# Moving GpSimd's copies of the global probabilities one slot on, and an output copy to an earlier place, in a fused attention and MoE kernel

## The chip, the cores and the metric

The kernel runs on one core of a Trainium2 chip. The metric is device time in microseconds (us) of one execution; the time before is 1080.44 us, the median of three runs (1079.32 to 1082.52). A core has five engines that run side by side, each through its own list of instructions in order: TensorE (PE, matmuls; its weight loads are PEld), VectorE (DVE), ScalarE (ACT), GpSimd (POOL), and SyncE (SP), which here only issues transfers (DMAs). They wait for each other by semaphores.

## The reference

```
def _attn_ref(q_l, k_l, v_l, q_g, k_g, v_g):       # B=8, H=8, 512 local and 32 global rows, D=64
    k_all = concat([k_g, k_l]); v_all = concat([v_g, v_l])
    out_g = softmax(scale * q_g @ k_all.T) @ v_all           # 32 global rows see all 544 keys
    s_ll = where(|i - j| <= 32, scale * q_l @ k_l.T, -1e9)   # local rows see a band
    s_lg = scale * q_l @ k_g.T                               # and the 32 global keys
    out_l = softmax(concat([s_lg, s_ll])) @ concat([v_g, v_l])
    return concat([out_g, out_l])
...
x = attention, as 4352 tokens x 512
out = (relu(x @ w_in) ** 2) @ w_out                # 512 -> 2048 -> 512
```

## The kernel before

The main loop (line 610) runs over 146 slots t. The first 128 slots each carry one half (256 local rows) of one head: scores on PE, a band softmax, a transpose of the probabilities, and their product with v. Slots t >= 9 also carry one eighth of an MoE block of 256 tokens: slot t works on step m = t - 9. A block is 8 steps; `gemm1(m)` makes 256 hidden columns, `act1` applies relu and square, and `gemm2(m-1)` adds the step before to two output tiles in PSUM (`o0` and `o1`), in two halves. So after each eighth step both output tiles must be emptied by `evac` (line 524) before the next `gemm2` may write them; this falls into slots with t % 8 = 2, in which `m % 8 == 1`. `evac` copies each tile with ACT to SBUF (`ot`) and sends it out. The copy of tile 0 goes into a buffer with the tag `ptl`, that of tile 1 into one with the tag `gvl`, and the global attention uses the same two buffers.

Most operands are split into a high and a low part of a rounded format, so that products take two or three matmuls; the low part is always a DVE subtraction of two SBUF tensors (`v`, `ph`, `ml`, `pl`, `qk`, `gvl`, `ptl`).

The probabilities of slot t are transposed by DMA. `turn(t)` (line 223) has POOL copy `prob` in three pieces to `planes`, low and high 16-bit halves apart, and SP issues a DMA transpose to `turned`. In slot t + 1, `join(t)` (line 231) has POOL put the halves together again in `joined`; `parts` (ACT, `ph`) and `parts_rest` (DVE: `ph`, `ml`, `pl`) split it, and PE multiplies (`av`, tile `xa`).

The rows of the global queries go the same way, for four heads at a time: 16 groups in all, two per 16 slots. Their scores are gathered in `sg` (128 rows x 640 columns: 544 keys, two repetitions of the last 32, and 32 of zeros). A group's work is spread over some eight slots by a table of jobs (line 685), each with a slot and a place in it. Before the change these are, counted from a slot d:

- d + 1: `g_soft` (DVE: row maximum) and `g_exp` (ACT)
- d + 2, place 3: `g_norm`: DVE repeats the 32 columns twice in `sg`, takes the reciprocal of the sum, and calls `g_turn`: one POOL copy of all of `sg` to `gp` (buffer tag `pth`), then a DMA transpose to `gq` (buffer tag `ptl`)
- d + 3, place 3: `g_split_v` (ACT `gvh`, DVE `gvl`), and `g_join`: one POOL copy of `gq` back to `sg`
- d + 4, place 3: `g_parts` (ACT `pth`, DVE `ptl` and the last part of `pth`); place 0: `g_av`, 13 matmuls to `gxo`, between the two halves of `gemm2`

d is 11 or 1 modulo 16. For d = 11 the slots of `g_norm`, `g_join` and `g_parts` are 13, 14 and 15 modulo 16; for d = 1 they are 3, 4 and 5.

From slot 17 on (`FREE`) every engine keeps the program order for what is issued through `pe`, `ve`, `ac`, `po` and `sp`; the planner puts the rest, among it the DMAs issued by `nc.sync` (the output, the global v and q), where it likes. In a slot POOL's order is: `join(t-1)`, `turn(t)`, then the jobs of place 3. ACT's is: `x_evac`, `split_v`, the two exponentials, `parts`, the jobs of place 3, `evac`, the split of the next q and k, `act1`, `act2`. SP's is: the transpose of `turn(t)`, the load of a later head, then a job's transpose.

Of the kernel before, what the change touches and what calls it, by code (L numbers as in the profile page):

```python
# [17 lines left out]
P = 128  # L18
# [9 lines left out]
NSTEP = NBLK * 8  # L28
# [10 lines left out]
def f(ap):  # L39
    return ap.bitcast(F32)  # L40
# [19 lines left out]
def attention_moe(  # L60
# [10 lines left out]
    pe, ve, ac, po, sp = (InOrder(tc, e) for e in (nc.tensor, nc.vector, nc.scalar, nc.gpsimd, nc.sync))  # L71
# [46 lines left out]
    sg = cp.tile([P, 2, 640], F32, name="sg")  # L118
# [36 lines left out]
    def scores(t):  # L155
        hd = heads[t]
        pool, tag = (ps_h, "h") if t < 8 and t % 2 else (ps_a, "s")
        s = pool.tile([P, 2, WIN], F32, tag=tag, name=f"s{t}")
        for u in range(2):
            qs, ks = slice(KC + u * P, KC + u * P + P), slice(128 * u, 128 * u + WIN)  # L160
            if plain(t):
                pe.matmul(s[:, u, :], hd["raw"][:, qs], hd["raw"][:, ks], start=True, stop=True)
            else:
                pe.matmul(s[:, u, :], hd["hi"][:, qs], hd["hi"][:, ks], start=True, stop=False)
                pe.matmul(s[:, u, :], hd["lo"][:, u * P : u * P + P], hd["hi"][:, ks], start=False, stop=True)
        hd["s"] = s
# [5 lines left out]
    def softmax1(t):  # L172
        hd = heads[t]
        hf = (t // 8) % 2
        pr = p2.tile([P, QK + QC], F32, tag="qk", name=f"pr{t}")[:, : 2 * WIN] if plain(t) else prob
        hd["pr"] = pr
        st = p2.tile([P, 8], F32, tag="st", name=f"st{t}")
        for u in range(2):
            m = 2 * hf + u
            ve.tensor_tensor_reduce(  # L180
                out=pr[:, WIN * u : WIN * (u + 1)],
                in0=hd["s"][:, u, :],
                in1=masks[:, WIN * m : WIN * (m + 1)],
                scale=-scale(t),
                scalar=3.0e38,
                op0=ALU.add,
                op1=ALU.min,
                accum_out=st[:, u : u + 1],
            )
        hd["st"] = st  # L190
# [40 lines left out]
    def join(t):  # L231
        words = joined.bitcast(U16).rearrange("p (n h) -> p h n", h=2)
        po.tensor_copy(words, turned.rearrange("p (h c) n -> p h (c n)", h=2))
# [44 lines left out]
    def x_evac(t):  # L278
        g, h = divmod(t, 8)
        xa = heads[t]["xa"]  # L280
        r = slice((h % 2) * 64, (h % 2) * 64 + 64)
        if g == 0:
            ac.copy(xg[r, h // 2, :], xa)
        else:
            ac.copy(x_h[r, g % 2, h // 2, :], xa)
            ve.tensor_sub(x_l[r, g % 2, h // 2, :], xa, f(x_h[r, g % 2, h // 2, :]))
        heads[t] = None
# [76 lines left out]

    def g_norm(t):
        s, st = sg[:, (t // 4) % 2, :], state["gst", t]
        for o in (544, 576):
            ve.tensor_copy(out=s[:, o : o + 32], in_=s[:, 512:544])
        ve.tensor_scalar(out=st[:, 3:4], in0=st[:, 2:3], scalar1=1e-9, scalar2=None, op0=ALU.add)
        ve.reciprocal(out=st[:, 0:1], in_=st[:, 3:4])  # L370
        ve.tensor_copy(out=st[:64, 1:2], in_=st[64:, 0:1])
        g_turn(t, s)

    def g_turn(t, s):

        a = p1.tile([P, 1280], U16, tag="pth", name=f"gp{t}")
        z = p1.tile([P, 10, P], U16, tag="ptl", name=f"gq{t}")
        words = s.bitcast(U16).rearrange("p (n h) -> p h n", h=2)
        po.tensor_copy(a.rearrange("p (h n) -> p h n", h=2), words)
        sp.dma_start_transpose(out=z, in_=a)  # L380
        state["gq"] = z

# [141 lines left out]
    def evac(blk, tiles=(0, 1)):  # L524
        for i in tiles:
            pool, tag = ((p1, "ptl"), (p1, "gvl"))[i]
            ot = pool.tile([P, DM], F32, tag=tag, name=f"ot{blk}_{i}")
            ac.copy(ot, moe["o"][i])
            if blk < NGR:
                b, hf = divmod(blk, 2)  # L530
                r0 = b * 544 + 32 + hf * 256 + i * P
                nc.sync.dma_start(out[r0 : r0 + P, :], ot)
            else:
                for bb in range(4):
                    r0 = (4 * i + bb) * 544
                    nc.sync.dma_start(out[r0 : r0 + 32, :], ot[32 * bb : 32 * bb + 32, :])
# [41 lines left out]
    def w_tick(t, place):  # L578
        if t < len(PLAN):
            for c in PLAN[t].split(",")[place]:  # L580
                {"b": w_pass, "s": w_chunk}[c]()
# [27 lines left out]
    jobs = {}  # L609
    for t in range(NSTEP + LAG + 1):  # L610
        m = t - LAG
# [10 lines left out]
            transposes(t - 1)  # L622
        if new:
            join(t - 1)
        if live and not early:
            scores(t)
        if old:
            pt_copy(t - 1)
        if NPLAIN <= t - 2 < NT:
            x_evac(t - 2)  # L630
        if live:
            softmax1(t)
        if run:
# [12 lines left out]
        for place in (4, 3):  # L646
            for job, *args in jobs.pop((t, place), ()):
                job(*args)
        if 0 < m <= NSTEP and m % 8 == 1 and m > 8:
            evac(m // 8 - 1)  # L650
        w_tick(t, 0)
        if live and early:
            g_scores(t)
# [29 lines left out]
        if live and t % 4 == 3 and (t // 8) % 2 == 1:  # L683
            d = t if t % 8 == 3 else t + 2
            for at, *job in (
                (d, 2, g_load_v, 0),
                (d + 1, 3, g_soft),
                (d + 1, 1, g_exp),
                (d + 2, 3, g_norm),
                (d + 3, 3, g_split_v, 0),  # L690
                (d + 3, 2, g_load_v, 1),
                (d + 3, 3, g_join),
                (d + 4, 3, g_parts),
                (d + 4, 0, g_av, 0),
                (max(d + 5, 17), 3, g_x, 0),
                (d + 5, 2, g_split_v, 1),
                (max(d + 6, 17), 0, g_av, 1),
                (max(d + 7, 18), 3, g_x, 1),
            ):
                place, job, *args = job  # L700
                jobs.setdefault((at, place), []).append((job, t, *args))
# [102 lines left out]
```

## Time and profile before

| | |
|---|---|
| median of the runs | 1080.44 us |
| the profiled execution | 1076.66 us |
| its span, first to last instruction | 1074.9 us |
| mean granted TensorE clock | 0.990 |
| PE busy | 1031.6 us (96%), 7040 matmul records |
| DVE busy | 853.1 us (79%) |
| ACT busy | 718.1 us (67%) |
| POOL busy | 382.1 us (36%), 496 instructions |

All times in the text are counted from the start of the span. "Busy" counts an engine's instructions from start to end, also where an instruction stands still because another engine holds something that it needs. Matmuls overlap and their ends are modelled, so the busy time of PE says less than the gaps and the lengths of the slots. A slot is measured here from the first matmul of `gemm1(m)` to that of the next step.

### The profile page before, as it was taken

The page shows a single profiled execution, that of the slowest core. Times are in us where ns is not written, and L with a number is a line of the kernel's source. Part 1 is how long each engine was busy: PE and PEld are TensorE (multiplying, and loading weights), DVE is VectorE, ACT ScalarE, POOL GpSimd, SP SyncE. Part 2 cuts the span into 40 slices and gives each one's busy share as a digit, 9 for nine tenths or more (in the row PEclk, how much of TensorE's full clock was granted, in tenths as well). Part 3 has the DMA queues.
Part 4 walks back from the last instruction along what each step waited for, and adds up shares of the span by engine and source line. Part 5 has one row for each costly group of instructions (what it writes and reads, how often), then busy time and mean ns, then how long its engine had stood idle before and what let it go on. Part 6 is the DMA issues. An engine that isn't in the chain of part 4 may idle for free.

```text
span 1074.9 us, 20570 instructions
## 1 busy us (share of the span) xinstructions
PE 1031.6 (96%) x7040; PEld 908.9 (85%) x7040; DVE 853.1 (79%) x2477; ACT 718.1 (67%) x1743; POOL 382.1 (36%) x496
## 2 busy tenths in 40 slices
PE   8999899999999999999999999999999999999998
PEld 6876788988988989888888989888888889889896
DVE  5689888888889878888879888888889888883211
ACT  6888667766767756767666766776667666664432
POOL 1010434444344443444335443453434343441000
PEclk9999999999999989999999999999999999999999
DMA  9772354545355444454445454445545453441000
GB/s 368 306 258 84 95 128 98 119 115 136 93 121 112 124 102 108 112 131 114 108 116 110 111 123 114 121 105 123 126 101 114 118 133 95 117 95 48 11 20 20
DMA packets 193576, 127.69 MB, mean 119 GB/s; under 512 B 143552, under 2 KB 168640, under 8 KB 193472
## 3 DMA queue, kind: packets, MB, share of 16 engines
q1 hardware_dynamic: 193328, 126.32, 45.8%
q8 instruction: 55, 0.90, 0.3%
q14 instruction: 49, 0.40, 0.1%
q10 hardware_dynamic: 144, 0.07, 0.0%
HBM read 82.84 MB, written 8.91 MB: 85 GB/s over the span
## 4 chain that ended last, share of the span: by engine, by line
PE 41%; DVE 30%; ACT 13%; issue 7%; DMA 5%; POOL 4%; POOLq 0%; SPq 0%; DVEq 0%; ACTq 0%
PE o L53 17%; PE h L53 16%; DVE qk L53 5%; ACT prob L53 5%; DVE prob L53 4%; DVE ml L53 4%; DMA turned<-planes 4%; PE xa L53 3%; PE s L53 3%; DVE gl L53 3%; POOL joined L53 2%; DVE st L53 2%; ACT ph L53 2%; DVE x_l L53 2%; POOL planes L53 2%
## 5 line engine op out<-in xcount | busy, mean ns | idle before, releaser
L53 PE MATMUL h<-x_h,ws 128*128 128x256 f32 x2048 | 395.6, 286 | 0.0
L53 PEld LDWEIGHTS h<-x_h,ws 128*128 128x128 f32 x2048 | 332.9, 194 | 0.7
L53 PE MATMUL o<-ws,gh 128*128 128x512 f32 x1024 | 323.9, 397 | 9.8 <-ACT ot L53 9.3
L53 PE MATMUL h<-x_l,ws 128*128 128x256 f32 x1024 | 293.0, 286 | 0.0
L53 POOL COPY joined<-turned 128x1024 uint16<-128x1024 uint16 x112 | 155.9, 1392 | 323.9 <-DMA turned<-planes 192.9
L53 POOL COPY planes<-prob 128x448 uint16<-128x448 uint16 x336 | 170.0, 543 | 211.6 <-DVE prob L53 211.6
L53 PEld LDWEIGHTS o<-ws,gh 128*128 128x128 f32 x1024 | 182.5, 188 | 44.7 <-ACT ot L53 12.8
L53 PE MATMUL o<-ws,gl 128*128 128x512 f32 x512 | 201.8, 394 | 0.0
L53 PEld LDWEIGHTS h<-x_l,ws 128*128 128x128 f32 x1024 | 199.3, 195 | 1.3 <-DVE x_l L53 0.2
L53 ACT ACTIVATE prob<-prob,st 128x224 f32<-128x224 f32 x224 | 106.3, 475 | 109.3 <-DVE st L53 109.2
L53 DVE TENSOR_TENSOR gl<-pt,gh 128x512 fp32r<-128x512 f32 x128 | 87.6, 684 | 75.9 <-ACT gh L53 75.2
L53 DVE TENSOR_TENSOR qk<-raw,qk 64x352 fp32r<-64x352 f32 x224 | 114.5, 511 | 7.5 <-ACT qk L53 0.6
L53 ACT CAST x_h<-xa 64x256 fp32r<-64x256 f32 x120 | 43.7, 364 | 113.5 <-PE xa L53 113.2
L53 PEld LDWEIGHTS o<-ws,gl 128*128 128x128 f32 x512 | 96.1, 188 | 22.8
L53 ACT ACTIVATE pt<-h 128x512 f32<-128x512 f32 x128 | 74.4, 581 | 57.0 <-PE h L53 56.3
L53 PE MATMUL s<-qk 128*128 128x224 f32 x448 | 85.9, 304 | 9.8 <-DVE qk L53 6.8
L53 ACT CAST ph<-joined 128x512 fp32r<-128x512 f32 x112 | 68.3, 610 | 27.7 <-POOL joined L53 26.9
L53 ACT CAST qk<-raw 128x608 fp32r<-128x608 f32 x112 | 78.3, 699 | 5.7 <-DMA raw<-in_pk_dram 5.3
L53 PEld LDWEIGHTS s<-qk 128*128 128x128 f32 x448 | 63.3, 194 | 20.4 <-DVE qk L53 19.7
L53 DVE CUSTOM_DVE_ANT_0 prob<-s,con 128x224 f32<-128x224 f32 x224 | 77.6, 382 | 3.3 <-PE s L53 1.3
L53 ACT ACTIVATE pt<-pt 128x512 f32<-128x512 f32 x128 | 74.5, 582 | 4.1
L53 ACT CAST gh<-pt 128x512 fp32r<-128x512 f32 x128 | 74.6, 583 | 2.4
(86 smaller groups left out, 1592.5 us busy)
## 6 DMA issues: line engine op xcount, KB each, us to landing
raw<-in_pk_dram SPq DMA_DIRECT2D x112, 400.0 KB, 3.5
wr<-in_w_dram SPq DMA_DIRECT2D x32, 512.0 KB, 7.9
gv<-in_vg_dram SPq DMA_DIRECT2D x32, 320.0 KB, 3.7
out_dram<-ot SPq DMA_DIRECT2D x32, 256.0 KB, 2.5
raw<-in_pk_dram SPq DMA_DIRECT2D x15, 432.0 KB, 8.4
qr<-in_qg_dram SPq DMA_DIRECT2D x31, 64.0 KB, 3.1
turned<-planes SPq DMA_TRANSPOSE x112, 3.1
out_dram<-ot SPq DMA_DIRECT2D x8, 64.0 KB, 1.7
```

Of the source, the lines that this page charges most:

```text
L53: r = method(*args, **kwargs)
```

## The change

Three things change. First, `g_turn` is no longer called by `g_norm`; it is a job of its own in slot d + 3, at a new place 6 at the head of the slot, right behind `join(t-1)` and ahead of `turn(t)`. `g_join` moves from slot d + 3, place 3, to slot d + 4, place 6. Second, DVE no longer repeats the 32 columns in `sg`; `g_turn` has POOL make four copies in place of one: the first 544 columns (both halves), the repeated columns once for each half by a read with a step of zero, and the last 32 columns. Third, `evac` is called once for each output tile: tile 0 behind `x_evac` and ahead of the softmax of the slot, tile 1 at the old place.

```
     def g_norm(t):
         s, st = sg[:, (t // 4) % 2, :], state["gst", t]
-        for o in (544, 576):
-            ve.tensor_copy(out=s[:, o : o + 32], in_=s[:, 512:544])
...
-        g_turn(t, s)
-
-    def g_turn(t, s):
+    def g_turn(t):
+
+        s = sg[:, (t // 4) % 2, :]
...
-        po.tensor_copy(a.rearrange("p (h n) -> p h n", h=2), words)
+        to = a.rearrange("p (h n) -> p h n", h=2)
+        po.tensor_copy(to[:, :, :544], words[:, :, :544])
+        for h in range(2):
+            twice = words[:, h, 512:544].unsqueeze(1).broadcast_to([P, 2, 32])
+            po.tensor_copy(to[:, h, 544:608].rearrange("p (k n) -> p k n", k=2), twice)
+        po.tensor_copy(to[:, :, 608:], words[:, :, 608:])
         sp.dma_start_transpose(out=z, in_=a)
...
             join(t - 1)
+        for job, *args in jobs.pop((t, 6), ()):
+            job(*args)
...
         if NPLAIN <= t - 2 < NT:
             x_evac(t - 2)
+        done = 0 < m <= NSTEP and m % 8 == 1 and m > 8
+        if done:
+            evac(m // 8 - 1, (0,))
         if live:
             softmax1(t)
...
-        if 0 < m <= NSTEP and m % 8 == 1 and m > 8:
-            evac(m // 8 - 1)
+        if done:
+            evac(m // 8 - 1, (1,))
...
                 (d + 2, 3, g_norm),
                 (d + 3, 3, g_split_v, 0),
                 (d + 3, 2, g_load_v, 1),
-                (d + 3, 3, g_join),
+                (d + 3, 6, g_turn),
+                (d + 4, 6, g_join),
                 (d + 4, 3, g_parts),
                 (d + 4, 0, g_av, 0),
```

## The prediction

> **What bounds the kernel now.** I read the page first: its busy times, then the groups for idle time of PE.
>
> ```profile
> span 1074.9 us, 20570 instructions
> PE 1031.6 (96%) x7040; PEld 908.9 (85%) x7040; DVE 853.1 (79%) x2477; ACT 718.1 (67%) x1743; POOL 382.1 (36%) x496
> L53 PE MATMUL o<-ws,gh 128*128 128x512 f32 x1024 | 323.9, 397 | 9.8 <-ACT ot L53 9.3
> ```
>
> PE is the bound on average, and its waits for the output copies `ot` come to 9.3 us. Next I cut the span into slots, since the average hides them. The columns of this view of stages are: stretch, its length, busy time of PE, PEld, DVE, ACT, POOL, granted clock, DMA share, GB/s.
>
> ```profile
> 296.93:303.88 6.95, 6.95 (x53) 6.37 (x51) 6.16 (x18) 4.99 (x15) 3.15 (x4) 1.00 0.31 83
> 303.88:311.75 7.87, 7.21 (x53) 6.40 (x51) 5.85 (x16) 5.51 (x14) 3.42 (x4) 1.00 0.53 130
> 325.68:333.25 7.57, 7.42 (x53) 6.51 (x51) 7.24 (x24) 5.36 (x15) 4.51 (x5) 1.00 0.48 101
> 333.25:341.76 8.51, 7.84 (x52) 6.52 (x51) 7.76 (x19) 5.15 (x12) 5.30 (x6) 1.00 0.68 141
> 341.76:349.51 7.75, 7.75 (x65) 7.13 (x64) 6.66 (x22) 5.70 (x16) 2.60 (x4) 1.00 0.44 106
> 364.34:371.74 7.40, 7.30 (x52) 6.47 (x51) 7.01 (x22) 6.32 (x16) 2.56 (x4) 1.00 0.62 141
> 371.74:379.35 7.61, 7.41 (x52) 6.51 (x51) 6.72 (x22) 5.47 (x14) 4.18 (x6) 1.00 0.51 132
> 379.35:389.59 10.24, 8.54 (x53) 7.04 (x51) 9.29 (x21) 5.15 (x12) 5.47 (x6) 0.92 0.59 129
> 389.59:399.65 10.06, 10.06 (x64) 9.44 (x64) 6.43 (x19) 5.46 (x14) 3.60 (x5) 0.74 0.40 102
> ```
>
> A slot without other work takes 6.95 us with PE full; with the 13 `gxo` matmuls 7.75 (row 5). Slots over that are: those with `evac` (7.87 and 7.40), and the two groups of slots with global work: 13 to 15 modulo 16 (rows 3 to 5; I call them stretch B) and 3 to 5 (the last three, stretch A). In rows 4 and 8 DVE is busy for 7.76 and 9.29 us, more than PE's own 6.95: there DVE sets the time. In row 9 PE ran at a clock of 0.74. The timeline of stretch B shows why DVE is slow:
>
> ```profile
> 319.69 1.64 POOL L53 COPY joined<-turned 128x1024 uint16<-128x1024 uint16 x1 [3.23 <-DMA turned<-planes]
> 320.63 0.73 DVE L53 TENSOR_SCALAR st<-st 128x2 f32<-128x2 f32 x1 [0.53 <-ACT prob L53]
> 330.28 1.64 POOL L53 COPY gp<-sg 128x1280 uint16<-128x1280 uint16 x1
> 330.84 1.92 DVE L53 TENSOR_TENSOR qk<-raw,qk 64x352 fp32r<-64x352 f32 x2
> 333.59 1.36 POOL L53 COPY joined<-turned 128x1024 uint16<-128x1024 uint16 x1 [1.67 <-DMA turned<-planes]
> 335.90 0.58 DVE L53 TENSOR_SCALAR prob<-prob,st 128x224 f32<-128x224 f32 x2
> 336.36 1.71 POOL L53 COPY planes<-prob 128x448 uint16<-128x448 uint16 x3 [1.41 <-DVE prob L53]
> 338.02 1.81 POOL L53 COPY sg<-gq 128x1280 uint16<-128x1280 uint16 x1
> 338.38 1.55 DVE L53 TENSOR_TENSOR ml<-joined,ph 64x128 fp32r<-64x128 f32 x1
> 340.30 0.98 DVE L53 TENSOR_TENSOR qk<-raw,qk 64x352 fp32r<-64x352 f32 x2
> 341.29 1.35 POOL L53 COPY joined<-turned 128x1024 uint16<-128x1024 uint16 x1 [1.45 <-DVE qk L53]
> 344.25 0.72 ACT L53 CAST pth<-sg 128x640 fp32r<-128x640 f32 x1
> 345.06 0.78 DVE L53 TENSOR_TENSOR ptl<-sg,pth 128x512 fp32r<-128x512 f32 x1 [0.21 <-issue]
> 346.27 0.22 PE L53 MATMUL gxo<-gvh,ptl 128*64 128x128 f32 x1
> ```
>
> A DVE instruction of this kind stands still until the POOL copy that is running ends. The `qk` pair takes 0.98 us alone and 1.92 while `gp` runs; the 64 x 128 `ml` takes 1.55 us and ends at 339.93, with `sg<-gq` ending at 339.83; even the two-column `st` stands until `joined` ends (321.36 after 321.33). So each long POOL copy of the global work costs DVE about 1 us wherever DVE has such work waiting.
>
> **The change, part by part.** *Output copies.* In slot 10 modulo 16, ACT and PE stand so:
>
> ```profile
> 304.74 0.49 ACT L53 ACTIVATE prob<-prob,st 128x224 f32<-128x224 f32 x1 [0.53 <-DVE st L53]
> 306.56 0.62 ACT L53 CAST ph<-joined 128x512 fp32r<-128x512 f32 x1 [0.78 <-POOL joined L53]
> 307.08 1.06 ACT L53 COPY ot<-o 128x512 f32<-128x512 f32 x2
> 307.71 0.73 PE L53 MATMUL o<-ws,gh 128*128 128x512 f32 x2 [0.66 <-ACT ot L53]
> 308.51 0.63 PE L53 MATMUL o<-ws,gh 128*128 128x512 f32 x2
> ```
>
> PE takes up `o0` at 307.71, when the first copy is done, and `o1` at 308.51. With tile 0 emptied three microseconds earlier, PE starts `o0` at once and `o1` when tile 1's copy, now first at 307.08, is done: 307.71 in place of 308.51, 0.80 us saved. In the other slot (7.40) all of the 0.45 over 6.95 goes. The moved copy (half of 1.06 us) falls into ACT's idle 0.53 before the exponentials, and the 0.78 before `ph` holds the rest; without that cover the softmax would start 0.5 us later and DVE with it. Over 7 slots of the first kind, 6 of the second and slot 18 (taken like the first) this makes 7 x 0.80 + 6 x 0.45 + 0.80 = 9.1; the page's row has 9.3, which I take. Bounds: 9.3, and 0 if DVE, which sets the time in the global slots that follow, takes it all back.
>
> *DVE's repeats and POOL's four copies.*
>
> ```profile
> 322.06 1.19 POOL L53 COPY planes<-prob 128x448 uint16<-128x448 uint16 x3 [0.73 <-DVE prob L53]
> L53 POOL COPY gp<-sg x16: 1253/1458/1729, 53.8 to 985.9; 128x1280 uint16<-128x1280 uint16 x16
> L53 POOL COPY sg<-gq x16: 1622/1801/2011, 58.3 to 990.3; 128x1280 uint16<-128x1280 uint16 x16
> L53 DVE COPY sg<-sg 128x32 f32<-128x32 f32 x32 | 8.3, 303 | 0.2 <-ACT sg L53 0.2
> ```
>
> DVE loses 2 x 0.303 = 0.6 us a group. Three copies of 896 elements together take 1.19 us undisturbed; at the 0.98 ns an element of one copy (1253 / 1280) they would take 0.88, so a further copy costs about 0.155. Four copies are then 1.25 + 3 x 0.155 = 1.72 us: the first 1.07 (1088 elements), the small ones 0.22 each. No row shows a read with a step of zero; between nothing extra and the cost of a copy of `sg<-gq` an element (1622 / 1280 = 1.27 ns) it is under 0.05 us, and I take nothing.
>
> *The moved copies, stretch B.* In slot 13 `gp` no longer meets `qk`: 0.94 us of DVE and the repeats go, `qk` ends in time, and the slot falls from 7.57 to 6.95. In slot 14 `joined` still runs 333.59 to 334.95, for its data land no earlier. DVE now reaches `v` before that and waits for it; `v` ends at 335.3. Then POOL's first copy holds the port until 336.4; `st`, which stood at about 335.3, goes behind it, and the three small copies alternate with `st` and the two scalings. These end at 337.6 in place of 336.48, and `planes` starts at 337.8, not 336.36: 1.4 later. The copy `sg<-gq` is gone from `ml` (-1.24), so `qk` ends where it did (341.1 against 341.28): slot 15 starts at 341.65, 0.1 earlier in all. But `planes` being 1.4 later, `turned` lands 1.4 later, and `joined` starts at 342.7, not 341.29. Now `g_join` comes behind it: 342.7 + 1.35, 0.35 for a waiting `v`, 1.65 for the copy, gives 346.05. Behind this wait, on ACT, `pth` and all that follows it in the slot (the split of q and k, relu, square), and on DVE `st`, the scalings and `ptl`: 346.05 + 0.2 + 0.2 + 0.65 for the softmax, then 0.78, gives 347.9. PE wants `ptl` at 346.27, less the 0.1: it waits 1.75. Stretch B: 23.83 (rows 3 to 5) - 0.1 + 1.75 = 25.5. Both ends: with no wait for `ptl` 23.7, and with the first copy held up by DVE as `joined` was in row 319.69 (1.64 for 1.35) twice over, 26.1.
>
> On SP the transpose of the group now stands ahead of that of `turn(t)` and of the head's load, where it stood behind both. It is issued at 337.8 and takes SP 1.33 us; the `planes` are done at 339.5, so the issue delays nothing; in the DMA engines it may (rival 3).
>
> *Stretch A* has the same edits, with more to lose in slots 3 and 4. I take it to last the same 25.5, for after the change the same chain (landing, `joined`, `g_join`, `pth`, `ptl`) ends last.
>
> ```profile
> sum 156.92, PE 145.95 PEld 128.17 DVE 132.78 ACT 96.38 POOL 75.39; mean PE 24.33 PEld 21.36 DVE 22.13 ACT 16.06 POOL 12.56
> sum 144.15, PE 138.11 PEld 121.04 DVE 130.58 ACT 97.01 POOL 72.79; mean PE 23.02 PEld 20.17 DVE 21.76 ACT 16.17 POOL 12.13
> ```
>
> These are the sums of six stretches A (from 248.91 on, 26.15 each) and six B (from 202.69 on, 24.03 each). A gains 0.65 six times, 3.9; its first, with the expert weights still to split, I set at 2.4, as the longest of the six (27.91, the last three rows of the stages, less 25.5). B loses 1.47 seven times, 10.3. **Sum:** -9.3 - 3.9 - 2.4 + 10.3 = -5.3 us against the profiled 1076.66 (span 1074.9 and 1.8 around it), 1071. The median of the runs is 3.8 higher than that execution, so I name 1075.
>
> **Rivals.** *1, much faster:* the copies fit into POOL's idle time. Row 336.36 has 1.41 us of it ahead of `planes`. If `st` goes ahead of the first copy, `planes` are not late and `qk` ends 1.2 earlier; `joined` comes at 341.3 and `g_join` ends at 344.65, `ptl` at 346.2 as before. Slot 15 starts at 340.4, PE wants `ptl` at 344.9 and waits 1.3: B is 340.4 - 325.68 + 7.75 + 1.3 = 23.8, bound by the landing, and A the same. That is -0.2 x 7 - 2.35 x 6 - 4.1 - 9.3 = -29, or 1051. For it: POOL is only 36% busy. Against it: in the rows above the waiting side always stood for a whole copy.
>
> *2, slower:* the clock. Row 8 has PE idle for 1.7 us (10.24 - 8.54), and in row 9 the clock fell to 0.74, which cost 2.3 us (10.06 against 7.75). Slot 333.25 with 0.67 us idle kept 1.00. The place is slots 5 and 15, the price 0.9 (mean of stretch A) to 2.3 us, and it decides from about 1.7 us of waiting for `ptl`, just what I get. At 1.3 in each of 14: +18, 1093. Against it: row 8's 1.7 us lay close together, and the waits here are split over two slots.
>
> The Trainium skill ("TensorE: Matmul & The Clock Gate", "Why this matters for your kernels") has the clock fall only after idle gaps of about 3 us, a whole window. By that rule this rival would give nothing, and the sum stays -5.3. This trace disagrees: 0.74 came behind 1.7 us.
>
> *3, slower:* the group's transpose, now ahead, delays `turned`.
>
> ```profile
> 554.41 1.39 POOL L53 COPY joined<-turned 128x1024 uint16<-128x1024 uint16 x1 [4.94 <-DVE prob L53]
> DMA to landing us min/median/max: 3.0/3.1/4.8
> DMA to landing us min/median/max: 2.9/4.8/6.1
> ```
>
> `turned` lands after 3.1 us (second row), at worst 4.8; `gq` (third row) alone 2.9, behind `turned` and a load 4.8. If the 1.9 of difference turns round, half of it, 0.9, goes into each wait for `ptl`: 14 x 0.9 = +12.6, 1088.
>
> **Numbers.** Forecast (1065 to 1083) 0.45, rival 1 0.2, rival 2 0.2, rival 3 0.15. Range 1049 to 1095: from rival 1 to rival 2, each with a little beyond. A change of 0.3%, 3.2 us, is about what a measurement can tell. Faster: 0.31 of the forecast, 0.2 and 0.02 = 0.53; same: 0.12 and 0.07 = 0.19; slower 0.28.
>
> **What would show it.** `o<-ws,gh` loses its wait for `ot`; `qk` and `ml` lose their 1.9 and 1.5; `st` or `prob` gain stretched instances; PE waits for `ptl` appear in slots 5 and 15, and slots 13 and 3 fall to 6.95. No wait for `ptl` would show rival 1, a clock under 0.9 in slots 5, 15 and after, rival 2; `turned` landing over 3.5 us, rival 3.

## The result, and the profile after

The changed kernel takes 1069.32 us (median of four runs, 1068.00 to 1071.19), the kernel before 1079.88 us in the runs that stand beside it. The ratio is 0.9899, with an interval of 0.9875 to 0.9923: about 10.6 us faster, where the prediction had 5.4 (1080.44 to 1075). The ratios leave out a few disturbed, slow executions, among them the profiled one of e5 below, which therefore has no column in the table of slots. The busy times of the kernel after, and the group in which PE's waits for the output copies stood:

```profile
PE 1029.5 (96%) x7040; PEld 902.3 (84%) x7040; DVE 867.7 (81%) x2445; ACT 721.5 (67%) x1743; POOL 385.0 (36%) x544
L53 PE MATMUL o<-ws,gh 128*128 128x512 f32 x1024 | 324.4, 398 | 3.2 <-ACT ot L53 3.0
```

PE's waits for `ot` fell from 9.3 to 3.0 us. DVE has 32 instructions fewer and is busy 14.6 us longer: its instructions stand still longer. The stages again, in the columns of the prediction (stretch, length, PE, PEld, DVE, ACT, POOL, granted clock, DMA share, GB/s): slots 10, 12, 13, 14, 15, then 2, 3, 4, 5 modulo 16 of the same round.

```profile
303.84:311.01 7.17, 7.17 (x52) 6.27 (x51) 5.85 (x16) 5.49 (x14) 3.43 (x4) 1.00 0.57 161
317.96:325.51 7.55, 7.43 (x52) 6.49 (x51) 7.19 (x20) 6.03 (x16) 2.65 (x4) 1.00 0.52 118
325.51:332.45 6.94, 6.94 (x52) 6.36 (x51) 6.61 (x22) 4.63 (x13) 2.76 (x4) 1.00 0.43 100
332.45:340.62 8.17, 7.80 (x52) 6.59 (x51) 7.88 (x19) 5.59 (x14) 4.72 (x8) 1.00 0.62 122
340.62:349.66 9.04, 8.20 (x66) 7.13 (x64) 8.69 (x22) 5.90 (x16) 4.74 (x5) 1.00 0.48 118
364.78:372.20 7.42, 7.33 (x53) 6.50 (x51) 7.03 (x22) 6.67 (x17) 2.56 (x4) 1.00 0.68 177
372.20:379.13 6.93, 6.93 (x52) 6.35 (x51) 6.01 (x22) 4.78 (x13) 2.75 (x4) 1.00 0.41 81
379.13:387.18 8.05, 7.66 (x53) 6.53 (x51) 7.31 (x19) 5.59 (x14) 5.32 (x8) 1.00 0.40 107
387.18:398.53 11.35, 9.73 (x65) 8.30 (x64) 8.69 (x20) 5.57 (x14) 5.89 (x6) 0.85 0.58 146
```

Slots 3 and 13 are free of the global work and stand at 6.94, slots 4 and 14 are shorter, slots 5 and 15 longer. Slot 10 fell from 7.87 to 7.17; slot 12, which nothing in the change touches, rose (row 2; it was 6.99). The last row holds a stretch at half clock, of which more below. The timeline of stretch B shows POOL's copies, what stands behind them on DVE, and PE's new wait:

```profile
334.48 1.74 POOL L53 COPY gp<-sg 128x1088 uint16<-128x1088 uint16 x4
334.66 1.05 DVE L53 TENSOR_SCALAR st<-st 128x2 f32<-128x2 f32 x1
336.49 1.71 POOL L53 COPY planes<-prob 128x448 uint16<-128x448 uint16 x3 [0.26 <-DVE prob L53]
341.45 1.36 POOL L53 COPY joined<-turned 128x1024 uint16<-128x1024 uint16 x1 [3.25 <-DMA turned<-planes]
342.72 1.75 POOL L53 COPY sg<-gq 128x1280 uint16<-128x1280 uint16 x1
342.88 1.61 DVE L53 TENSOR_SCALAR st<-st 128x2 f32<-128x2 f32 x1
344.50 0.73 ACT L53 CAST pth<-sg 128x640 fp32r<-128x640 f32 x1 [1.04 <-POOL sg L53]
345.26 1.04 DVE L53 TENSOR_TENSOR ptl<-sg,pth 128x512 fp32r<-128x512 f32 x1
346.35 0.27 PE L53 MATMUL gxo<-gvh,ptl 128*64 128x128 f32 x1 [0.74 <-DVE ptl L53]
```

In this stretch `ml` and `qk` no longer meet a global copy. In their place the two-column `st` stands behind it, 1.05 us and 1.61 us; it ends at 335.71 and 344.49, with the first piece of `gp` and with `sg<-gq` (342.72 + 1.75 = 344.47). PE's wait for `ptl` is in the last row. The groups show the exchange over the whole kernel (behind the bar: busy time, mean ns of one); before, `st` had a mean of 246 and `ml` of 517 ns:

```profile
L53 DVE TENSOR_SCALAR st<-st 128x2 f32<-128x2 f32 x128 | 62.5, 488 | 34.0 <-ACT prob L53 29.8 <-ACT pr L53 4.0
L53 DVE TENSOR_TENSOR ml<-joined,ph 64x128 fp32r<-64x128 f32 x112 | 34.2, 305 | 3.5
```

For a longer view I measured every slot, by the start of its first `gemm1` matmul, in the profiled execution of each kernel. The table gives mean lengths in us over slots 22 to 117 (six of each kind); A is slots 3 + 4 + 5, B is 13 + 14 + 15; the last line is the sum of slots 18 to 21, the first stretch A, which is not in the means. The kernels e1 to e12 are the experiments of the next section.

```
slot   before  after   e1     e2     e3     e4     e6     e8     e9    e10    e11    e12
 1      7.88   8.20   7.87   8.19   7.87   7.95   8.28   7.91   8.29   8.15   7.87   7.91
 2      7.61   7.52   7.57   7.61   7.64   7.53   7.55   7.51   7.53   7.55   7.56   7.17
 3      7.57   6.94   7.63   6.94   7.17   6.94   6.94   7.12   7.12   6.94   7.57   7.57
 4      9.92   8.03   9.93   8.05   8.94   9.07   8.06   8.96   7.66   8.05  10.11  10.12
 5      8.66   9.41   8.67   9.06   8.98   8.50   8.84   8.22   8.70   7.91   8.57   8.66
10      8.27   7.58   7.58   8.57   8.30   7.58   7.63   7.53   7.54   7.42   8.25   7.53
12      7.04   7.43   7.41   7.14   7.06   7.37   7.38   7.41   7.43   7.40   6.95   7.00
13      7.75   6.94   7.78   6.94   7.30   6.94   6.94   7.31   7.24   6.94   8.46   8.77
14      8.52   8.19   8.52   8.15   8.52   9.25   8.35   8.53   7.25   8.13   8.52   8.46
15      7.75   9.04   7.75   9.01   7.75   8.37   8.90   7.75   8.71   7.94   7.75   7.75
A      26.15  24.39  26.24  24.05  25.09  24.52  23.83  24.30  23.48  22.90  26.25  26.35
B      24.02  24.17  24.05  24.11  23.57  24.56  24.19  23.59  23.21  23.01  24.73  24.97
18-21  36.97  38.99  38.39  38.72  37.90  38.98  39.01  39.73  37.12  38.41  36.82  38.35
```

From before to after, A gives 1.76 six times, B takes 0.15 six times, slot 10 gives 0.69, slot 12 takes 0.39 and slot 1 takes 0.32. (Slot 1 grows so in every kernel of the table with `g_join` moved; no run separates why.) All of slots 22 to 117 come to -9.1 us (741.6 to 732.5), slots 18 to 21 to +2.0, the rest to +1.4; the sum is the -5.8 us between the two spans (1074.9 and 1069.1).

The runs differ by 10.6, the profiled executions by 5.5 (1076.66 and 1071.19). The granted clock goes with the rest. The four runs of the kernel after had mean granted clocks of 0.994 to 0.998 (the profiled one 0.994); 50 runs of the kernel before beside the experiments had 0.982 to 0.992. Within one kernel, a run with 0.001 less is 0.79 us longer (one slope fitted to the runs of all kernels, each about its own mean).

### The profile page after: what moved, and what is told of

It reads as the page before. It is cut to its first block, busy times and chain, and to the rows that moved or that the text cites. A ratio compares the mean times of both kernels' runs of the same rounds, so it can differ in the third digit from the quotient of the medians.

```text
span 1069.1 us, 20564 instructions
## 1 busy us (share of the span) xinstructions
PE 1029.5 (96%) x7040; PEld 902.3 (84%) x7040; DVE 867.7 (81%) x2445; ACT 721.5 (67%) x1743; POOL 385.0 (36%) x544
## 4 chain that ended last, share of the span: by engine, by line
PE 43%; DVE 37%; ACT 8%; issue 5%; DMA 3%; POOL 2%; SPq 0%; DVEq 0%; POOLq 0%; ACTq 0%
PE o L53 17%; PE h L53 16%; DVE prob L53 6%; DVE st L53 5%; DVE qk L53 5%; PE xa L53 4%; ACT prob L53 3%; DVE v L53 3%; PE s L53 3%; DVE gl L53 2%; PE gxo L53 2%; DVE x_l L53 2%; DVE ph L53 2%; DVE pl L53 2%; DMA raw<-in_pk_dram 2%
## 5 line engine op out<-in xcount | busy, mean ns | idle before, releaser
L53 PE MATMUL h<-x_h,ws 128*128 128x256 f32 x2048 | 391.4, 284 | 0.0
L53 PEld LDWEIGHTS h<-x_h,ws 128*128 128x128 f32 x2048 | 329.1, 192 | 0.7
L53 PEld LDWEIGHTS h<-x_l,ws 128*128 128x128 f32 x1024 | 197.0, 192 | 3.2 <-DVE x_l L53 2.6
L53 DVE TENSOR_TENSOR qk<-raw,qk 64x352 fp32r<-64x352 f32 x224 | 109.1, 487 | 8.7 <-ACT qk L53 1.6
L53 PE MATMUL s<-qk 128*128 128x224 f32 x448 | 83.5, 298 | 8.2 <-DVE qk L53 5.6
L53 DVE TENSOR_SCALAR st<-st 128x2 f32<-128x2 f32 x128 | 62.5, 488 | 34.0 <-ACT prob L53 29.8
L53 DVE TENSOR_TENSOR v<-raw,v 128x192 fp32r<-128x192 f32 x112 | 80.5, 719 | 0.0
```

The costliest lines, as they stand in the source:

```text
L53: r = method(*args, **kwargs)
```

## The experiments

The measured times, each against the kernel before on the same chip. "At one clock" is the difference of the means to the kernel before, with both moved to a clock of 0.990 by the slope of 0.79 us; it is an estimate, and I use it for differences of several us only. (For the change itself "before" is the profiled execution's clock, and the difference is taken to the three values of the kernel before at 0.990 beside the experiments, 1079.1 to 1080.0.)

```
kernel                                    median    ratio [95%]              clock  before  us at one clock
after, the change                        1069.32   0.9899 [0.9875, 0.9923]   0.996   0.990  -5 to -6
e1   output copies alone                 1077.70   0.9948 [0.9928, 0.9968]   0.989   0.986     -3.3
e2   after, without the output copies    1071.81   0.9903 [0.9880, 0.9926]   0.995   0.986     -3.7
e3   repeats alone                       1068.32   0.9857 [0.9827, 0.9886]   0.990   0.986    -12.6
e4   after, g_join at its old place      1072.80   0.9901 [0.9871, 0.9931]   0.988   0.986    -10.0
e5   after, repeats on DVE again         1070.04   0.9903 [0.9881, 0.9925]   0.996   0.989     -4.7
e6   after, gxo matmuls later            1067.10   0.9884 [0.9862, 0.9906]   0.997   0.989     -6.4
e8   repeats + output copies, no move    1064.17   0.9853 [0.9830, 0.9876]   0.991   0.989    -14.0
e9   e8 + g_join moved + gxo later       1060.21   0.9816 [0.9794, 0.9837]   0.996   0.989    -14.1
e10  after, g_join cut to 64 columns     1050.97   0.9721 [0.9701, 0.9741]   0.996   0.987    -23.1
e11  before, maximum over 32 columns     1083.09   1.0017 [0.9998, 1.0036]   0.989   0.987     +3.5
e12  e11 + output copies                 1079.80   0.9990 [0.9972, 1.0009]   0.987   0.987     -1.4
```

### The three parts, each by itself: e1, e2, e3

e1 is the kernel before with the third part of the change:

```
+        done = 0 < m <= NSTEP and m % 8 == 1 and m > 8
+        if done:
+            evac(m // 8 - 1, (0,))
         if live:
             softmax1(t)
...
-        if 0 < m <= NSTEP and m % 8 == 1 and m > 8:
-            evac(m // 8 - 1)
+        if done:
+            evac(m // 8 - 1, (1,))
```

> The kernel before with only the output copies taken apart (tile 0 behind x_evac, tile 1 at the old place). Theory A (the prediction's own term): the 9.3 us that PE waits for ot are gained in full, the ratio to the kernel before is 0.991. Theory B (read from the profile after, where slots 10 modulo 16 became 0.69 us shorter, slots 2 not at all and slots 12 longer by 0.4 to 0.6): DVE sets the time in the slots that follow and takes most of it back; 7 x 0.69 - 7 x 0.45 = 1.7 us, ratio 0.998, and PE's wait for ot in the profile is gone all the same.

Measured: 0.9948, 1077.70 against 1083.47, between the two theories. Slot 12 of e1, in the view of stages:

```profile
319.44:326.91 7.47, 7.39 (x52) 6.49 (x51) 7.14 (x19) 5.95 (x16) 2.57 (x4) 1.00 0.53 119
```

Slot 10 gains its 0.69 on average, and two slots later 0.37 of it are gone: DVE is busy for 7.14 of the 7.47 us of slot 12. Slot 2 keeps its length (7.61 and 7.57), so the wait for `ot` that ended there had hidden another. Slots 22 to 117 together give 1.5 us (741.6 to 740.2), where the term of the prediction has some 7.5 of its 9.3 for them. The timed gain is 5.7 us, 3.3 of it at one clock; the profiled execution of e1 doesn't show it (span 1075.4), so what made the rest stays open.

e2 is the kernel after with both output tiles emptied at the old place: the first two parts alone.

```
-        if done:
-            evac(m // 8 - 1, (0,))
...
         if done:
-            evac(m // 8 - 1, (1,))
+            evac(m // 8 - 1)
```

> The kernel after with both output tiles emptied at the old place, so only the changes to the global work are left. Theory A: they are worth 4 us or nothing, as the prediction's sum has it (ratio 0.996 to 1.004). Theory B: they carry most of the gain, 8 to 10 us, ratio 0.991 to 0.992; slots 3 and 13 fall to 6.95 us, slot 4 from 10.2 to 8.0, and slots 5 and 15 take 9.0 in place of 7.75 with PE waiting for ptl and pth.

Measured: 0.9903, as theory B has it. The whole change has 0.9899, so the output copies, worth 0.5% alone, add nothing that these runs can tell to the other two parts. In the table slot 10 is back at 8.57.

e3 is the kernel before with the second part alone: DVE's two repeats go, and POOL makes its four copies where it made one, behind `turn(t)`.

```
-        for o in (544, 576):
-            ve.tensor_copy(out=s[:, o : o + 32], in_=s[:, 512:544])
...
-        po.tensor_copy(a.rearrange("p (h n) -> p h n", h=2), words)
+        to = a.rearrange("p (h n) -> p h n", h=2)
+        po.tensor_copy(to[:, :, :544], words[:, :, :544])
+        for h in range(2):
+            twice = words[:, h, 512:544].unsqueeze(1).broadcast_to([P, 2, 32])
+            po.tensor_copy(to[:, h, 544:608].rearrange("p (k n) -> p k n", k=2), twice)
+        po.tensor_copy(to[:, :, 608:], words[:, :, 608:])
```

> The kernel before with only the repeats of the columns moved: DVE's two copies gone, GpSimd's four copies at the old place behind turn(t). Theory A (a POOL copy holds DVE for as long as it runs): the first copy of about 1.1 us stands in for the one of 1.25 to 1.73, DVE's ml or qk is held by 0.2 to 0.4 us less and the repeats are gone: 0.3 to 0.8 us a group, -3 to -9 us, ratio 0.992 to 0.997. Theory B (what POOL does more, 0.47 us a group, falls on the chain): +0 to +4 us, ratio 1.000 to 1.004.

Measured: 0.9857, 15 us, beyond both theories and more than the whole change. So something in the whole change is a loss. The two profiled executions are less far apart, 8.2 us (spans of 1074.9 and 1066.7), and slots 22 to 117 give 8.8; some 3 us of the 15 are clock (0.990 for 0.986), and what there is beyond that isn't in the traces. The timelines of slots 3 and 4 show where so small an edit gets its gain. Before:

```profile
251.91 0.63 DVE L53 COPY sg<-sg 128x32 f32<-128x32 f32 x2
253.47 1.22 DVE L53 TENSOR_TENSOR ml<-joined,ph 64x128 fp32r<-64x128 f32 x1
256.55 1.26 DVE L53 TENSOR_TENSOR qgz<-qr,qgz 128x128 fp32r<-128x128 f32 x1
```

and e3:

```profile
253.90 0.37 DVE L53 TENSOR_TENSOR ml<-joined,ph 64x128 fp32r<-64x128 f32 x1
254.08 2.59 POOL L53 COPY gp<-sg 128x1088 uint16<-128x1088 uint16 x4
254.63 1.76 DVE L53 TENSOR_TENSOR qk<-raw,qk 64x352 fp32r<-64x352 f32 x2
256.91 0.29 DVE L53 TENSOR_TENSOR qgz<-qr,qgz 128x128 fp32r<-128x128 f32 x1
257.35 1.36 POOL L53 COPY joined<-turned 128x1024 uint16<-128x1024 uint16 x1 [0.68 <-DVE qgz L53]
```

Without the 0.63 us of repeats DVE runs ahead of POOL: `ml` starts before `gp` and is through in 0.37 us, and `qgz` is through before `joined` begins (0.29 for 1.26). But the `qk` pair now meets `gp` and takes 1.76 us, where 0.98 is its time alone. In the means over the six stretches `ml` falls by 0.71 us in slot 3 and 0.57 in slot 13, and `qk` takes 0.63 and 0.47 of it back. What is left is the length of the repeats, and in slot 4 `qgz` (1.12 to 0.29). By the table of slots, slot 3 falls 0.41, slot 4 0.97 and slot 13 0.45, while slot 5 takes 0.32: five of its six run at a clock of 0.82 or 0.83, with half-clock windows that lay partly in slot 4 before.

### Which of the moves costs: e4, e8, e9, and the repeats under the move: e5

e4 is the kernel after with `g_join` put back:

```
-                (d + 4, 6, g_join),
+                (d + 3, 3, g_join),
```

> The kernel after with g_join back at slot d + 3, place 3, that is ahead of join in POOL's order and as soon as gq has landed. Theory A (the wait of PE for ptl in slots 5 and 15 is the price of g_join standing behind join): these slots fall from 9.0 to 7.75 us, and g_join now runs while DVE does qk, gl and x_l of slots 4 and 14, of which only qk can be held, 0 to 0.9 us: -5 to -16 us against the kernel after, ratio to the kernel before 0.975 to 0.985. Theory B (a POOL copy costs DVE its full length wherever it stands): slots 4 and 14 become longer by 1.2 us as slots 5 and 15 become shorter, ratio 0.988 to 0.992, no change against the kernel after.

Measured: 0.9901, as theory B has it. `g_join`'s place makes no difference to the total; it moves the loss. Slots 14 and 15 of e4, and what meets in 14:

```profile
333.41:342.89 9.48, 7.84 (x53) 6.64 (x51) 9.19 (x19) 5.58 (x14) 6.86 (x10) 0.99 0.61 134
342.89:352.08 9.19, 9.19 (x65) 8.57 (x64) 7.01 (x22) 5.79 (x16) 3.86 (x5) 0.82 0.48 134
```

```profile
340.09 2.25 DVE L53 TENSOR_TENSOR qk<-raw,qk 64x352 fp32r<-64x352 f32 x2
340.51 1.61 POOL L53 COPY sg<-gq 128x1280 uint16<-128x1280 uint16 x1 [1.37 <-DMA gq<-gp]
```

PE no longer waits for `ptl`, but `gq` now lands late in the slot and its copy holds `qk` for 2.25 us, where 0.98 is its time alone. DVE sets slot 14 (9.19 busy of 9.48), PE stands idle for 1.6 us, and the clock falls to 0.82 in the slot behind. The mean granted clock of e4's runs is 0.988, the kernel after's 0.996. At one clock e4 would be some 4 us ahead of the kernel after (last column of the table).

e8 is the change without both moves: e3 and e1 together. Against the kernel after:

```
+        g_turn(t, s)
...
-    def g_turn(t):
+    def g_turn(t, s):
...
-                (d + 3, 6, g_turn),
-                (d + 4, 6, g_join),
+                (d + 3, 3, g_join),
```

> The kernel before with the repeats moved to GpSimd at the old place and the output copies taken apart: the change without its moves by a slot. Theory A (the parts add up): 0.9857 and 0.9948 give 0.981 (0.978 to 0.984); moving g_turn and g_join is then a loss of 8 to 10 us within the change, and slots 13 to 15 take 23.6 us in place of 24.2. Theory B (the output copies give nothing on top, since DVE has no room in the slots behind them): 0.985 to 0.988. Theory C (the moves are needed for the rest to count): 0.990, like the kernel after.

Measured: 0.9853, 1064.17, as theory B has it. Against the kernel after (0.9899; the intervals just touch) the two moves cost about 5 us, and some 8 at one clock, for the clock is higher with them (0.996 for 0.991). The same two edits, without the output copies and on one chip, are e2 and e3, and they differ by the same 0.0046. Against e3 (0.9857) the output copies are again worth nothing that shows. Slots 14 and 15 of e8:

```profile
332.58:341.10 8.52, 7.85 (x52) 6.53 (x51) 7.88 (x19) 5.17 (x13) 5.31 (x6) 1.00 0.73 137
341.10:348.85 7.75, 7.75 (x65) 7.13 (x64) 6.67 (x22) 5.70 (x16) 2.61 (x4) 1.00 0.46 113
```

Slot 15 has PE full at 7.75, with no wait for `ptl`; slot 14 still pays for `g_join` on `ml`.

e9 then combines what the runs so far favour: `g_turn` at its old place behind `turn(t)`, `g_join` at the new one, and the first `gxo` matmuls 0.7 us later, between the two output tiles of the second half of `gemm2`. Against the kernel after:

```
+        g_turn(t, s)
...
-                (d + 3, 6, g_turn),
                 (d + 4, 6, g_join),
                 (d + 4, 3, g_parts),
-                (d + 4, 0, g_av, 0),
+                (d + 4, 8 if d + 4 >= 17 else 0, g_av, 0),
...
-            gemm2(m - 1, 1)
+            gemm2(m - 1, 1, (0,))
+            for job, *args in jobs.pop((t, 8), ()):
+                job(*args)
+            gemm2(m - 1, 1, (1,))
```

> The kernel before with the repeats on GpSimd and g_turn at the old place, g_join behind join at the head of slot d + 4 as in the change, the output copies taken apart, and the first gxo matmuls 0.7 us later. Theory A (g_turn at the new place is what holds st and the scalings; g_join at the new place no longer holds ml in slots 4 and 14, and its price is PE's wait for ptl, of which 0.7 us go): slots 13 to 15 take 7.3 + 7.2 + 8.4 = 22.9 us in place of 24.2 of the kernel after, ratio to the kernel before 0.970 to 0.977. Theory B (DVE is held for the length of the copy wherever it stands): slots 4, 5, 14 and 15 together stay what they are in the run without the moves, ratio 0.981 to 0.986.

Measured: 0.9816, 1060.21: the fastest of the kernels that leave nothing out, 9 us under the change. Its slots 14, 15 and 4:

```profile
329.40:336.66 7.26, 7.21 (x53) 6.42 (x51) 6.63 (x19) 5.04 (x13) 3.07 (x4) 1.00 0.56 132
336.66:345.35 8.69, 8.21 (x66) 7.14 (x64) 8.37 (x20) 6.05 (x17) 4.74 (x5) 1.00 0.44 115
375.32:382.99 7.67, 7.42 (x52) 6.49 (x51) 6.76 (x20) 5.31 (x13) 3.08 (x4) 1.00 0.56 136
```

With `g_join` gone from slots 14 and 4, and no `g_turn` at their head, they are at 7.26 and 7.67; B is 23.21 and A 23.48, 0.4 and 0.8 under e8's. Part of the gain over e8 is the clock, 0.996 for 0.991; by the last column of the table the two are alike. So neither theory holds whole: the time is in the range of theory B, but slots 4, 5, 14 and 15 together did fall against e8 (33.46 to 32.32), and slots 14 and 15 came near theory A (7.25 and 8.71 for 7.2 and 8.4).

e5 is the kernel after with DVE's repeats and POOL's one copy again, at the new place:

```
+        for o in (544, 576):
+            ve.tensor_copy(out=s[:, o : o + 32], in_=s[:, 512:544])
...
-        to = a.rearrange("p (h n) -> p h n", h=2)
...
-        po.tensor_copy(to[:, :, 608:], words[:, :, 608:])
+        po.tensor_copy(a.rearrange("p (h n) -> p h n", h=2), words)
```

> The kernel after with only the repeats undone: DVE copies the 32 columns twice in g_norm again, and GpSimd makes one copy of all columns at the new place. Theory A (the repeats on DVE are most of the loss, as the run with them alone moved says, because what DVE does behind them slips into the next joined copy): slots 3 and 13 go from 6.94 to about 7.3 us or more, 0.4 to 0.8 us a group: +5 to +11 us against the kernel after, ratio to the kernel before 0.995 to 1.000. Theory B (the repeats cost only where gp stood right behind them and held DVE; with gp moved to the next slot DVE has the room, and one copy holds it a little longer than the first of four, 0.2 us): +0 to +3 us against the kernel after, ratio 0.990 to 0.993.

Measured: 0.9903, as the kernel after and as theory B has it. The repeats, worth 1.4% at the old place of `g_turn`, are worth nothing that shows once it has moved. This rests on the times alone. A reading that fits, but isn't shown: after the move there is no `gp` in slots 3 and 13, and PE, not DVE, sets their time (6.94 of 6.94 us; DVE 6.01 and 6.61), so 0.6 us of DVE has room. The sum can't have both parts.

### The wait for ptl: e6, e10

e6 is the kernel after with the later `gxo` matmuls of e9's diff (the line with `g_av` and the piece in front of `av`).

> The kernel after with the first half of the gxo matmuls put between the two tiles of the second half of gemm2, 0.7 us later for PE. Theory A (PE's wait for pth and ptl is 1.2 to 1.3 us in slots 5 and 15 and nothing else is late there): those slots fall by 0.7 us each, 14 x 0.7 = -10 us against the kernel after, ratio to the kernel before 0.980 to 0.983. Theory B (the wait goes on to xa, since gxs must empty the shared PSUM tile behind gxo before av, and DVE's ph, ml and pl are late too): -3 us or nothing, ratio 0.987 to 0.990.

Measured: 0.9884, within the interval of the kernel after, and as theory B has it. Five of the six slots 15 go from 9.01 to 8.70 us or so (the mean, 8.90, holds one of 9.80), and slots 0 and 1 behind them take 0.19 and 0.08 back. So the 0.7 us of later matmuls recover some 0.3, and the wait turns up elsewhere: PE's waits for `ptl` fall from 9.4 to 5.1 us, and those of its weight loads for `gxs`, ahead of `xa`, rise from 1.7 to 7.9.

e10 is the kernel after with `g_join` copying 64 of the 640 columns:

```
-        po.tensor_copy(words, z.rearrange("p (h c) n -> p h (c n)", h=2))
+        po.tensor_copy(words[:, :, :64], z.rearrange("p (h c) n -> p h (c n)", h=2)[:, :, :64])
```

> The kernel after, with g_join putting together only 64 of the 640 columns of the global probabilities (the rest of sg keeps older values, so the global rows' results are left out in part); its copy is then about 0.3 us in place of 1.75, and all else stands where it is. Theory A (PE's wait for pth and ptl in slots 5 and 15, and st's 1.6 us there, are the length of this copy): slots 5 and 15 fall from 9.0 to 7.75 us, 14 x 1.25 = -17 us against the kernel after, ratio to the kernel before 0.973 to 0.976. Theory B (the wait is for the landing of turned and for joined, which planes late behind g_turn delay): g_join's length is not on the path, slots 5 and 15 stay over 8.7 us, ratio 0.986 to 0.990.

Measured: 0.9721, 1050.97, as theory A has it: the length of that one copy is worth some 19 us (0.9899 less 0.9721, of 1080). Slot 15 of e10, and the copy with the `st` behind it:

```profile
336.65:344.41 7.76, 7.76 (x65) 7.12 (x64) 7.29 (x22) 5.80 (x16) 3.43 (x5) 1.00 0.57 138
```

```profile
338.79 0.43 POOL L53 COPY sg<-gq 128x128 uint16<-128x128 uint16 x1
338.95 0.30 DVE L53 TENSOR_SCALAR st<-st 128x2 f32<-128x2 f32 x1
```

The copy takes 0.43 us for 1.75, `st` 0.30 for 1.61, and slot 15 is back at 7.76 with PE full, while slot 14 stays as in the kernel after (8.13 and 8.19). So the growth of slots 5 and 15 hangs on the length of `g_join`'s copy: with the rest of the chain as it was, it is gone.

### Who takes the output copies' gain back: e11, e12

Both kernels take the row maximum of the global scores over 32 columns in place of 544, which frees DVE in slots 12 and 2; e12 has e1's edit as well.

```
-        ve.tensor_reduce(out=st[:, 0:1], in_=s[:, :544], op=ALU.max, axis=AX.X)
+        ve.tensor_reduce(out=st[:, 0:1], in_=s[:, :32], op=ALU.max, axis=AX.X)
```

> The kernel before, with g_soft's maximum taken over the first 32 columns and not over all 544 (the exponentials' shift is then that of a part of the row, the search over the rest is left out): 0.55 us less for DVE in slots 2 and 12 modulo 16. Both theories: slots 2 and 12 have their time from PE or from the wait for ot in this kernel (7.4 and 6.95 to 7.05 us), so little comes of it: -0 to -4 us, ratio 0.996 to 1.000. It is the base for the next.

> The same with the output copies taken apart, so that the two differ by that alone. Theory A (what the output copies gave in slot 10 was taken back in slot 12, and in slot 2 nothing came of it, because DVE had g_soft's 0.72 us there): with DVE relieved, slot 12 stays at 7.0 us, slot 10 falls by 0.69 and slot 2 from 7.4 to 6.95 to 7.1: 7 x 0.69 + 6 x 0.4 = -7 us against the run before it, ratio to the kernel before 0.988 to 0.992. Theory B (the output copies' gain is that of the run with them alone, whatever DVE has to do): 0.9948 less what the first of the two gains, and slot 12 is longer by 0.4 us all the same.

Measured: 1.0017 and 0.9990; the intervals overlap, and both miss what was expected (0.996 to 1.000, and 0.988 to 0.992). Slot 13 of e11:

```profile
327.09:335.25 8.16, 7.79 (x52) 6.54 (x51) 7.23 (x23) 5.39 (x15) 4.02 (x6) 1.00 0.62 119
```

and of e12:

```profile
329.24:337.75 8.51, 7.85 (x52) 6.54 (x51) 7.59 (x24) 5.38 (x15) 4.01 (x5) 1.00 0.65 118
```

With DVE relieved, slot 12 keeps its length (6.95 and 7.00 in the table), and slot 2 falls with the edit, in the mean from 7.56 to 7.17, as the term had it: DVE was what stood behind the wait there. But the next slot, 13, takes 0.35 in the rows above and 0.31 in the mean: the loss moved on by one slot. Slots 22 to 117 give 2.7 us of the 6.7 that slots 10 and 2 gain. A shorter reduction alone makes the kernel no faster: slot 13 is 0.71 longer than before. In its row above `st` stands behind `joined` (0.76 us) and `ml` behind `gp` (1.22), where in the kernel before `v` (1.11) and `qk` (1.92) did; why that costs more stays open.

## Why the prediction was right or wrong

The predicted 1075 is 5.7 above the median, inside the range, and on the right side. Point by point:

**The sum and its base.** The sum gave 1071 for a profiled execution, and the profiled execution of the kernel after took 1071.19. That it was met is luck. The four terms were -9.3, -3.9, -2.4 and +10.3; the slots gave -2.4 (10, 2 and 12 together), -10.6, +2.0 and +0.9 (six of the seven stretches B), and slot 1 and all the rest added 1.9 and 2.4 that no term had. The errors cancel. The last step failed too, "the median of the runs is 3.8 higher than that execution": for the kernel after the median is 1.9 lower. The distance of one profile from the runs was carried over as if it belonged to the kernel. Most of it was clock: the profiled execution of before had 0.990 for some 0.987 in the other runs (at 0.79 us per 0.001, 2.4 of the 3.8), that of after 0.994 for 0.996 (1.6 of the 1.9). So the gain came out at 10.6 us where 5.4 was forecast.

**Output copies, -9.3.** Mis-sized. Slot 10 gained 0.69 (0.80 was forecast), slot 2 0.09 (0.45). PE's waits for `ot` did fall by 6.3, but DVE took 0.39 back in slot 12 and stood behind the wait in slot 2 (7.03 of 7.42 us). The lower bound, 0 if DVE takes it back, was nearer: alone 3.3 us at one clock, on top of the rest nothing that the ratios can tell (e8 against e3, after against e2; 1.4 and some 2 us at one clock). The bound named the right engine, and the choice between the ends should have looked at the busy DVE of slot 12.

**Repeats, -0.6 a group.** The duration was right (0.63). Their worth depends on the place: alone, by the slots of e3, 0.45 a group in stretch B, where `qk` takes back what `ml` gains, and 1.06 in stretch A, where `qgz` no longer stands behind `joined`; with the move nothing that shows (e5). POOL's four copies took 1.74 us (1.72 forecast). Of a strided read with step zero, taken as free, the rows show no extra price.

**Stretch B, +1.47 each.** The mechanism was right at each place: slot 13 fell to 6.94, `st` stood behind the first piece of `gp`, PE waited for `ptl`. The handovers were each too long. Slot 14 was to last 9.0 us (332.63 to 341.65) and lasts 8.17: `gp` follows `joined` at once, ahead of `v`'s end, so `st` is free at 335.71 (336.4 forecast), and `planes` starts at 336.49, not 337.8, as the small pieces run beside the reciprocal and the scalings. `joined` follows at 341.45 (342.7 forecast), `ptl` ends at 346.30 (347.9). PE's wait was to be 1.75 and slot 15 grew by 1.29. The gaps of the trace show 0.74 of that for `ptl` and some 0.1 for `pth`; but matmul ends are modelled, and by the starts of the matmuls the two hold PE up for 0.90 and 0.27. B grew by 0.15: -0.81, -0.33 and +1.29 in its three slots. Over the kernel the waits of PE for `ptl`, counted by the semaphore, are 13 (time, instructions, mean):

```profile
PE gxo L53 <- DVE ptl L53: 9.4, 13, 0.7
```

**Stretch A, -0.65 each, and the first -2.4.** Assumed equal to B. The six gained 1.76 each: 0.63 in slot 3 and 1.88 in slot 4, where `gp` and `sg<-gq` no longer meet DVE's longest slot, less 0.75 in slot 5. That 0.75 is two things. The wait for `ptl` and `pth` costs slot 5 what it costs slot 15: five of the six last 9.01 to 9.04 us at full clock, for 7.75 in the kernel before. But there only two of the six had full clock; four, with half-clock windows, took 8.54 to 10.06, and that is gone. The first stretch went the other way: slots 18 to 21 grew by 2.0 (slot 19 fell by 1.63, 20 and 21 rose by 1.55 and 2.11). The step "the issue delays nothing" fails here. On SP, before and after:

```profile
135.94 0.33 SPq L53 DMA_DIRECT2D raw<-in_pk_dram  x1
```

```profile
136.03 1.32 SPq L53 DMA_TRANSPOSE gq<-gp  x1
137.44 0.53 SPq L53 DMA_DIRECT2D raw<-in_pk_dram  x1
141.21 0.70 ACT L53 CAST qk<-raw 128x608 fp32r<-128x608 f32 x1 [3.51 <-DMA raw<-in_pk_dram]
```

The head's load is issued 1.5 us later, behind the moved transpose, and ACT waits 3.51 us for it (1.68 before). The five profiled kernels with `g_turn` moved have a slot 20 of 12.03 to 12.28 us, the others 10.47 to 11.70. Behind it slot 21 has PE full, but at a clock of 0.76, where it was 1.00 before:

```profile
143.75:153.62 9.87, 9.87 (x65) 9.24 (x64) 7.31 (x20) 6.07 (x16) 3.73 (x5) 0.76 0.32 82
```

Slot 21 is long in e1 and e8 too (9.25 and 10.13), which move no global copy to another slot, so how much of the 2.0 is the load's is not shown.

**Rival 1**, everything fits into POOL's idle time: no. `st` did stand behind the copy. **Rival 3**, the transpose delays `turned`: no. `turned` lands after 3.1 us in the median as before (over 3.5 us, the sign named, 10 of 112 times for 6), and `gq` faster (before: median 4.8). Landings of `turned` and of `gq` after:

```profile
DMA to landing us min/median/max: 3.0/3.1/5.1
DMA to landing us min/median/max: 2.9/3.0/3.5
```

**Rival 2**, the clock falls behind the wait for `ptl`: right as a mechanism, wrong as an outcome. It happened once (in the first stretch A the half clock came behind the wait for the load). Two windows of 3.41 us in slot 53 of the kernel after:

```profile
390.85:394.26 3.41, 1.79 (x15) 1.14 (x14) 2.93 (x5) 2.45 (x5) 2.78 (x4) 1.00 0.03 7
394.26:397.68 3.42, 3.42 (x16) 2.73 (x15) 2.75 (x7) 1.40 (x4) 0.51 (x1) 0.50 0.75 170
```

In the first PE is idle for 1.6 us, the waits for `pth` and `ptl` of this slot, and the next has half the clock. The wait shows as 0.84 us of idle PE in the stretch B above, too little. About 1.7 us, the point named, fits this window but is no rule, as the last section shows. Against it, the long slot 4 that had brought the clock down in the kernel before is gone: five windows at half clock in slots 22 to 117 before, one after. The rival was looked for on the losing side alone, while the change was taking the same price off.

## What to carry to other kernels

An instruction that runs ahead of another engine's copy is worth more or less than its own length by what it pushes into the copy: the same 0.6 us brought 0.45, 1.06 or nothing. Parts that relieve the same stretch don't add, so each should be timed alone before both are kept. A wait removed is worth what the next slots' busiest engine leaves of it. And a profile's distance from the median isn't a property of the kernel: compare the granted clocks before carrying it over.

## What the runs showed of the hardware

The half-clock stretches of the traces of before and after last 3.41 or 6.83 us, so the clock goes by windows of 3.41 us. A window with PE busy for 1.79 of 3.41 us was followed by one at half rate (slot 53 above). So it went in the kernel before, but not in every such window:

```profile
384.53:387.95 3.42, 1.90 (x13) 1.17 (x11) 3.31 (x6) 1.82 (x4) 2.79 (x3) 1.00 0.38 74
387.95:391.36 3.41, 3.23 (x15) 2.88 (x15) 2.78 (x9) 1.70 (x7) 1.34 (x1) 0.50 0.79 223
555.20:558.61 3.41, 1.62 (x7) 1.35 (x8) 1.64 (x4) 2.74 (x6) 1.96 (x4) 1.00 0.23 77
558.61:562.02 3.41, 3.41 (x29) 3.09 (x28) 1.97 (x6) 1.82 (x4) 1.36 (x1) 1.00 0.96 205
```

An idle time of 1.5 us in the window was enough in the first pair, and 1.8 us was not in the second. Between 30 and 1010 us, PE is busy for less than 0.6 of the window in seven windows of the kernel before and four of the kernel after; five and two of them are followed by half clock. What tells them apart stays open. The Trainium skill, "TensorE: Matmul & The Clock Gate", "Why this matters for your kernels", has the clock fall behind idle gaps of over about 3 us, a whole window. The first pair disagrees.

The runs of one kernel scatter with the granted clock: of the kernel before, beside e8, 1077.08 us at 0.992 and 1083.14 at 0.985. That is an estimated four half-clock windows between two executions of one program (0.007 of 1080 us, over half of 3.41 us); what decides how many there are, these runs don't show.

A two-column `st`, with one operand in SBUF, can stand still for nearly a whole POOL copy: 1.61 us behind the 1.75 of `sg<-gq`, 0.30 behind the 0.43 of e10's. The Trainium skill, "SBUF — State Buffer", "Who interferes with whom", says that an instruction of this kind can take the port pair that VectorE and GpSimd share, that the pair is held for a whole instruction, and that the later one waits; the trace agrees.
